# A gated MLP's u half: seven block products instead of eight for two of three chunk pairs

## The chip, the cores and the metric

One core of a Trainium2 chip runs the whole program. The metric is the device time of one execution in microseconds (us), the median over runs. The engines are TensorE (PE; its weight loads are listed as PEld), VectorE (DVE), ScalarE (ACT), GpSimd (POOL) and SyncE (SP), which issues the DMA transfers. Each engine takes its instructions in the order in which they were queued, and waits at an instruction until what that one needs is there.

## The reference

Windowed attention feeds an FFT mixing layer with an MLP, and that feeds a gated MLP. The change touches the last stage, and in it the product with the first half of `w_in`:

```python
def _moe2_ref(x, w_in, g_ln, w_sg, b_sg, w_out):      # x: 4 x 576 x 512, w_in: 512 x 1024
    h = x @ w_in
    c = np.float32(np.sqrt(2.0 / np.pi))
    h = 0.5 * h * (1.0 + np.tanh(c * (h + 0.044715 * h ** 3)))
    u, v = (h[..., :512], h[..., 512:])
    mu = np.mean(v, axis=-1, keepdims=True)
    var = np.mean((v - mu) ** 2, axis=-1, keepdims=True)
    v_n = (v - mu) / np.sqrt(var + 1e-06) * g_ln
    v_s = np.einsum('ts,bsd->btd', w_sg, v_n) + b_sg[None, :, None]
    gated = u * v_s
    return (x + gated @ w_out).astype(np.float32)
```

## The kernel before

**Numbers.** Every fp32 operand of a product is split into a hi and a lo part (`xh`, `xl` for the tokens), and one product of 128 by 128 by some columns is three matmuls, hi by hi, hi by lo, lo by hi (`mm3`, L124 to L126). Weights come from HBM as 64-bit words that `raw` (L158 on ACT, L159 and L160 on DVE) turns into fp32 and `halves` splits (L164 on ACT; L165 on DVE, or on POOL once the MLP is over).

**Stages.** Attention and the FFT come first, then the MLP. Its larger part, `wino`, works on pairs of token chunks (a chunk is 384 of the 2304 tokens; there are six): `quad` makes a two by two block product from seven block products instead of eight (Strassen's scheme in Winograd's form), with the sums on the side of the output made by DVE and POOL (L830, L831), relu and split by ACT and DVE (L824, L825), and `units` multiplies by the second weight and adds the result to `uT`, the fp32 tokens, in `done` (L878, a DVE add whose one operand is a PSUM bank). Then the gated MLP:

- `split_x` splits the six chunks: for each chunk and each of four 128-row blocks k, ACT writes hi (L900) and POOL writes lo, which is token minus hi (L901). That is 24 splits on each of the two engines. The tiles are called `xh`/`xl` (chunk 0), `xhm`/`xlm` (chunks 1 and 2) and `xht`/`xlt` (chunks 3 to 5).
- `gate_u` (the u half): for each chunk and each of four output blocks f, 4 blocks k by 3 matmuls of 384 columns into a PSUM bank (called `c` or `g`), then a gelu on ACT (L1008) that writes over `uT`. That is 6 x 4 x 12 = 288 matmuls.
- `v_tiles` (the v half, token-major, with the layer norm), `spatial` (the mixing by `w_sg`, whose weights `load_sg` brings) and `project`.

**What sets the order.** The program is written as generators that a driver interleaves by credit (`drive`, with lanes for weight decoding), and a tile scheduler then puts the instructions of each engine in a fixed order. In `wino` a lane decodes `w1`, `w2` and, from its fourth pair on, the gated MLP's `w_in` (`at("in", ...)`). `split_x` is issued after the last relu splits of the MLP (`issue_after`). Work with high priority, such as `done`, goes ahead of what was written earlier.

**Banks.** PSUM has eight banks. When `gate_u` begins, it takes banks that the last `units` still hold: a bank is free when DVE's `done` add has read it.

Of the kernel before, what the change touches and what calls it, by code (L numbers as in the profile page):

```python
# [1 line left out]

# [31 lines left out]
GSETS = (3, 4, 5, 7, 8, 6, 1, 2)  # L34
# [73 lines left out]
class Kernel:  # L108
# [70 lines left out]
    def decode_w1(self, f):  # L179

        V = self.nc.vector
        w = self.aps["w1"]
        a21 = self.raw(w[f + 1], 0)
        yield 0
        a22 = self.raw(w[f + 1], 256)
        self.halves(a22, *self.w1_block(f, 4))
        s1 = self.pers.tile([128, 256], I32, tag="dec_w", bufs=4, name="dec_w")[:].bitcast(F32)
        V.tensor_tensor(out=s1, in0=a21, in1=a22, op=ALU.add)
        self.halves(s1, *self.w1_block(f, 5))
        yield 0  # L190
# [25 lines left out]
    def gset(self, i):  # L216
        return self.sets[GSETS[i]]

    def decode_in(self, uv, kc):
        i = 4 * uv + kc  # L220
        t = self.gset(i // 2)
        yield from self.decode(self.aps["wi"][i], t[:, 2 * (i % 2)], t[:, 2 * (i % 2) + 1])

    def decode_out(self, kc):
        t = self.gset(4 + kc // 2)
        yield from self.decode(self.aps["wo"][kc], t[:, 2 * (kc % 2)], t[:, 2 * (kc % 2) + 1])

    def w_in(self, uv, kc):
        t = self.gset(2 * uv + kc // 2)
        return t[:, 2 * (kc % 2)], t[:, 2 * (kc % 2) + 1]  # L230

    def w_out(self, kc):
        t = self.gset(4 + kc // 2)
        return t[:, 2 * (kc % 2)], t[:, 2 * (kc % 2) + 1]
# [713 lines left out]
    def open_gmlp(self):  # L948
# [46 lines left out]

    def gate_u(self):
# [114 lines left out]
def emit(tc, aps):  # L1111
    with ExitStack() as ctx:
# [263 lines left out]
```

## Time and profile before

| | us |
|---|---|
| median of 3 runs | 771.15 (770.38 to 771.23) |
| the profiled execution, its time | 772.72 |
| its span, first to last instruction | 770.9 |
| PE busy | 750.4 (97% of the span) |
| DVE, ACT, POOL busy | 486.0, 340.6, 219.7 |
| granted TensorE clock, mean | 0.997 of full speed |

Durations below are from the profiled execution. How to read its views: busy time adds up the durations of an engine's instructions; the chain of waits goes back from the last instruction, at each step to what released it; a timeline lists an engine's instructions by start, and a row with "x4" stands for four alike in a row, its time being that from the first's start to the last's end. Matmuls overlap in PE, so the step from start to start is what a matmul costs, not its duration of 0.33 to 0.35 us.

### The profile page before, as it was taken

What the parts mean: (1) busy time and instruction counts of PE and PEld (TensorE: products, weight loads), DVE (VectorE), ACT (ScalarE), POOL (GpSimd) and SP (SyncE); (2) the same over time, 40 slices, a digit from 0 to 9 for tenths busy, and PEclk for the clock granted to TensorE, in tenths of its full rate; (3) what the DMA queues carried; (4) which work ended last, traced back from release to release, by engine and by line L of the source; (5) the groups of instructions that cost most, each with busy time, mean ns of one, the idle gap of its engine ahead of it and who ended that gap; (6) DMA issues with size and microseconds to landing.
All of it is one profiled execution on the core that took longest, in us unless ns stands there. A gap on an engine that the chain in (4) does not pass through costs nothing.

```text
span 770.9 us, 13909 instructions
## 1 busy us (share of the span) xinstructions
PE 750.4 (97%) x5018; PEld 723.3 (94%) x5018; DVE 486.0 (63%) x1382; ACT 340.6 (44%) x811; POOL 219.7 (28%) x278
## 2 busy tenths in 40 slices
PE   7899899899999999999999999999999999999998
PEld 6789788899999999999999999999999998989898
DVE  4668876883445599884688657645700468574662
ACT  5687986745235555341245324323732333231210
POOL 2244454524213460065421112022690021010100
PEclk9999999999999999999999999999999999999999
DMA  9997762343015888585838914853310020104023
GB/s 265 307 291 229 210 212 68 111 136 116 8 29 180 278 270 297 181 321 178 309 122 308 363 81 162 336 205 123 121 57 1 0 71 22 62 23 142 11 72 122
DMA packets 84772, 123.37 MB, mean 160 GB/s; under 512 B 24416, under 2 KB 61664, under 8 KB 84704
## 3 DMA queue, kind: packets, MB, share of 16 engines
q1 hardware_dynamic: 82912, 119.13, 46.4%
q0 software_dynamic: 576, 2.97, 1.1%
q8 instruction: 39, 0.64, 0.3%
q10 hardware_dynamic: 1216, 0.39, 0.2%
q14 instruction: 29, 0.24, 0.1%
HBM read 91.79 MB, written 30.67 MB: 159 GB/s over the span
## 4 chain that ended last, share of the span: by engine, by line
PE 90%; DVE 5%; ACT 3%; DMA 1%; issue 1%; SPq 0%; POOL 0%; ACTq 0%; DVEq 0%; POOLq 0%
PE w L124 7%; PE w L126 7%; PE w L125 7%; PE g L124 7%; PE g L126 6%; PE g L125 6%; PE c L124 6%; PE c L125 6%; PE c L126 6%; PE acc L126 3%; PE acc L125 3%; PE h L124 3%; PE h L125 3%; PE acc L124 3%; PE h L126 3%; PE sc L314 3%
## 5 line engine op out<-in xcount | busy, mean ns | idle before, releaser
L164 ACT ACTIVATE set<-dec_w 128x256 fp32r<-128x256 f32 x103 | 41.9, 414 | 63.2 <-PE w L125 29.4
L831 POOL TENSOR_TENSOR u<-u 128x384 f32<-128x384 f32 x15 | 17.7, 1179 | 158.6 <-ACT u L830 99.6
L605 POOL TENSOR_TENSOR rq<-rq,mhalf 128x1 f32<-128x1 f32 (+1 forms) x24 | 15.7, 654 | 157.8 <-DVE rq L604 155.6
L321 ACT ACTIVATE s<-s,mx 128x128 f32<-128x128 f32 x144 | 47.6, 392 | 7.7 <-DVE mx L319 7.5
L158 ACT ACTIVATE dec_g<-dec_s 128x256 f32<-128x256 f32 x88 | 37.4, 428 | 30.5 <-DMA dec_s<-in_wi 15.3
L125 PE MATMUL acc<-rl,set 128*128 128x384 f32 x144 | 48.7, 338 | 0.0
L126 PE MATMUL acc<-rh,set 128*128 128x384 f32 x144 | 48.6, 337 | 0.0
L319 DVE CUSTOM_DVE_ANT_0 s<-sc,mask 128x128 f32<-128x128 f32 x144 | 33.4, 285 | 22.0 <-PE sc L314 13.8
L124 PE MATMUL acc<-rh,set 128*128 128x384 f32 x144 | 46.3, 337 | 0.0
L314 PE MATMUL sc<-k,q 128*128 128x128 f32 x288 | 41.0, 286 | 5.0 <-DVE mx L319 2.4
L165 DVE TENSOR_TENSOR set<-dec_w,set 128x256 fp32r<-128x256 f32 x83 | 37.8, 462 | 10.8 <-ACT set L164 4.3
L160 DVE SCALAR_TENSOR_TENSOR dec_w<-dec_g,dec_w 128x256 int32<-128x256 int32 x88 | 42.1, 481 | 3.5 <-ACT dec_g L158 2.8
L1037 DVE BATCH_NORM_STATS2 st<-u 128x6 f32<-128x512 f32 x18 | 12.4, 691 | 48.7 <-ACT u L1033 48.7
L314 PEld LDWEIGHTS sc<-k,q 128*128 128x128 f32 x288 | 36.7, 198 | 6.7 <-DVE mx L319 3.0
L831 DVE TENSOR_TENSOR u<-w,u 128x384 f32<-128x384 f32 x44 | 24.3, 552 | 27.2 <-POOL u L831 22.4
L159 DVE TENSOR_SCALAR dec_w<-dec_s 128x256 int32<-128x256 int32 x88 | 32.3, 373 | 6.1 <-DMA dec_s<-in_wi 3.2
L878 DVE TENSOR_TENSOR uT<-g,uT 128x384 f32<-128x384 f32 x36 | 19.4, 554 | 26.4 <-PE g L126 26.3
L703 DVE SCALAR_TENSOR_TENSOR rl<-h,rh 128x384 fp32r<-128x384 f32 x36 | 19.8, 551 | 23.1 <-ACT rh L702 23.1
L341 PEld LDWEIGHTS pv<-v,pts 128*64 128x64 f32 x576 | 23.5, 137 | 9.3 <-issue 4.2
L341 PE MATMUL pv<-v,pts 128*64 128x65 f32 x576 | 29.1, 226 | 2.8 <-ACT s L321 2.4
L830 ACT ACTIVATE u<-w 128x384 f32<-128x384 f32 x29 | 14.0, 484 | 38.0 <-PE w L126 37.1
L688 DVE TENSOR_TENSOR uT<-acc,uT 128x384 f32<-128x384 f32 x48 | 25.4, 549 | 5.3 <-PE acc L126 4.9
(359 smaller groups left out, 2632.5 us busy)
## 6 DMA issues: line engine op xcount, KB each, us to landing
dec_s<-in_w SPq DMA_DIRECT2D x64, 256.0 KB, 3.4
v<-in_v SPq DMA_DIRECT2D x16, 520.0 KB, 5.5
xht<-xb SPq DMA_DIRECT2D x10, 768.0 KB, 8.5
xhm<-xb SPq DMA_DIRECT2D x10, 768.0 KB, 7.9
xlm<-xb SPq DMA_DIRECT2D x8, 768.0 KB, 8.9
k<-in_k SPq DMA_DIRECT2D x11, 512.0 KB, 6.3
xf<-u SPq DMA_DIRECT2D x18, 256.0 KB, 3.0
p<-xf SPq DMA_DIRECT2D x24, 192.0 KB, 3.2
```

What stands on the lines that cost most here:

```text
L124: mm(out, lhsT=lh, rhs=rh, start=first and i == 0, stop=False)
L125: mm(out, lhsT=lh, rhs=rl, start=False, stop=False)
L126: mm(out, lhsT=ll, rhs=rh, start=False, stop=last and i == n - 1)
L158: nc.scalar.activation(out=g, in_=s[:, :, 1].bitcast(F32), func=AF.Prelu, scale=2.0 ** -112, alpha=-2.0 ** 32)
L160: nc.vector.scalar_tensor_tensor(out=w, in0=g[:].bitcast(I32), scalar=3, in1=w, op0=ALU.logical_shift_left, op1=ALU.bitwise_or)
L164: self.nc.scalar.activation(out=hi, in_=f, func=AF.Copy)
L165: (self.nc.gpsimd if self.bp is None else self.nc.vector).tensor_tensor(out=lo, in0=f, in1=hi, op=ALU.subtract)
L314: nc.tensor.matmul(sc[:, hp], lhsT=q[:, hp].rearrange("p a b -> p (a b)"), rhs=k[:, hp, o:o + 128], start=True, stop=True)
L319: nc.vector.tensor_tensor_reduce(out=s[:, hp], in0=sc[:, hp], in1=mask, scale=-0.125, scalar=1e30, op0=ALU.add, op1=ALU.min, accum_out=mx[ ...
L321: nc.scalar.activation(out=s[:, hp], in_=s[:, hp], func=AF.Exp, bias=mx[:, hp:hp + 1], scale=-1.0)
L341: nc.tensor.matmul(o[r:r + 64, i // 4, 65 * (i % 4):65 * (i % 4) + 65], lhsT=pts[:, i // 2, 64 * (i % 2):64 * (i % 2) + 64], rhs=v[:, 65 * ...
L831: add = lambda eng, o, i, j: eng.tensor_tensor(out=o, in0=i, in1=j, op=ALU.add)
```

## The change

**The products.** Chunks 0 and 1 keep the plain form (`gplain`, 48 matmuls each). Chunks 2 and 3, and 4 and 5, are taken as pairs: `gquad(p, f)` makes two output blocks by two chunks from seven block products of two blocks k, each 6 matmuls. Two pairs by two halves f by seven by 6 are 168 matmuls; with the plain 96 they are 264, where there were 288. `TURNS` sets the order of the seven. Products 1 and 6 have no bank of their own: they are accumulated onto the bank of product 0 and of product 5, after ACT or DVE has read these (`skip`). The other sums on the output side are five DVE adds (L1049) and an ACT copy (L1065) for each `gquad`.

**The sums of tokens.** Four of the seven products multiply sums of tokens. `tsum` makes them from `uT` (four DVE subtractions for each pair and block k, L1020), and `tsplit` splits them (hi on ACT, L1031; lo on DVE, L1032). For the first pair this is done between the splits of chunk 0 and of the other chunks; for the second pair the sums are made before `gquad(1, 1)` and split within it.

**The weights.** `wi` for the u half is stored in blocks, and `decode_u` makes seven forms of it for each half f, as `decode_w1` does (L193 to L202 before), with one block more that `gplain` needs. So 16 blocks are split where 8 were. Of `w_in`'s v half two of four row blocks are still decoded in `wino`, one (with one of `w_out`) beside `gate_u`, one before `gquad(2, 1)`; the other three row blocks of `w_out` are decoded in the first `spatial`. `load_sg` of the first block comes after `gate_u`. The tiles of v for batch 0 come after `gate_u`, in turns with `gplain(1)`.

```diff
-GSETS = (3, 4, 5, 7, 8, 6, 1, 2)
+FORMS = ((5, 3, 7, 4, 0, 1, 2, 6), (7, 4, 5, 0, 3, 2, 1, 6))
+TURNS = (0, 2, 3, 5, 1, 4, 6)
+W_V = ((8, 0, 8, 1), (8, 2, 8, 3), (6, 0, 6, 1), (3, 0, 3, 1))
+W_OUT = ((3, 2, 3, 3), (5, 0, 5, 1), (6, 2, 6, 3), (5, 2, 5, 3))
+SG = (1, 4, 7)
...
-    def mm3(self, out, terms, first=True, last=True):
+    def mm3(self, out, terms, first=True, last=True, skip=False):
 
         n = len(terms)
         for i, (lh, ll, rh, rl) in enumerate(terms):
-            mm = self.nc.tensor.matmul
+            mm = partial(self.nc.tensor.matmul, skip_group_check=skip)
...
+    def u_block(self, f, i):
+        n = 8 * f + FORMS[f].index(i)
+        t = self.flat((3, 4, 5, 7)[n // 4])[:, 512 * (n % 4):512 * (n % 4) + 512]
+        return t[:, 0:256], t[:, 256:512]
+
+    def decode_u(self, f):
+        return self.decode_forms(self.aps["wi"], 2 * f, lambda i: self.u_block(f, i), True)
+
+    def decode_forms(self, w, f, place, spare=False):
 
         V = self.nc.vector
-        w = self.aps["w1"]
         a21 = self.raw(w[f + 1], 0)
+        if spare:
+            self.halves(a21, *place(7))
...
+    def tsum(self, p, k, ts):
+
+        sub = lambda o, a, b: self.nc.vector.tensor_tensor(out=o, in0=a, in1=b, op=ALU.subtract)
+        t1, t2, t3, t4 = ts
+        m, n = 2 * p, 2 * p + 1
+        sub(t1, self.xk(n, k), self.xk(m, k))
+        sub(t2, self.xk(n, k + 2), t1)
+        sub(t3, self.xk(n, k + 2), self.xk(n, k))
+        sub(t4, self.xk(m, k + 2), t2)
+        return {5: t1, 2: t2, 3: t3, 4: t4}
+
+    def tsplit(self, i, k, t):
+        h, l = self.tb[i][k]
+        self.nc.scalar.activation(out=h, in_=t, func=AF.Copy)
+        self.nc.vector.tensor_tensor(out=l, in0=t, in1=h, op=ALU.subtract)
+
+    def tsums(self, p, temps):
+        for k in range(2):
+            f = self.tsum(p, k, [t[:, 0:384] for t in temps])
+            for i in (2, 3, 5, 4):
+                self.tsplit(i, k, f[i])
...
+        x = lambda c, o: [(self.xh[c][:, o + k], self.xl[c][:, o + k]) for k in range(2)]
+        tb = {0: x(m, 0), 1: x(m, 2), 6: x(n, 2), **self.tb}
+        p1, u3, p5 = (self.ptile("u") for _ in range(3))
+        add = lambda o, i, j: V.tensor_tensor(out=o, in0=i, in1=j, op=ALU.add)
+
+        def gelu(e, t, c):
+            A.activation(out=self.xk(2 * p + t, 2 * f + e), in_=c, func=AF.Gelu_apprx_tanh)
+
+        banks = {}
+        for i in TURNS:
+            hi, lo = self.u_block(f, i)
+            if i in (1, 6):
+                o = banks[i // 6 * 5]
+            else:
+                o = banks[i] = self.ctile()[:, 0:384]
+            self.mm3(o, [(hi[:, 128 * k:128 * k + 128], lo[:, 128 * k:128 * k + 128], *tb[i][k]) for k in range(2)], first=i not in (1, 6), skip=i in (1, 6))
+            if then is not None and i in self.tb:
+                then(i)
+            if i == 0:
+                A.activation(out=p1, in_=o, func=AF.Copy)
+            elif i == 1:
+                gelu(0, 0, o)
+            elif i == 2:
+                add(p1, o, p1)
+            elif i == 3:
+                add(u3, o, p1)
+            elif i == 4:
+                add(u3, o, u3)
+                gelu(1, 0, u3)
+            elif i == 5:
+                add(p5, o, u3)
+                gelu(1, 1, p5)
+            else:
+                add(p1, o, p1)
+                gelu(0, 1, p1)
+            yield 960
...
+        temps = [self.cp.tile([128, 512], F32, tag=f"t{i}", name="temp")[:, 0:384] for i in range(4)]
+        yield from self.gplain(0)
+        yield from self.gquad(1, 0)
+        late = [self.tsum(2, k, t) for k, t in enumerate((temps, [self.ptile("p") for _ in range(4)]))]
+        yield from self.gquad(1, 1, lambda i: [self.tsplit(i, k, late[k][i]) for k in range(2)])
+        yield from self.gquad(2, 0)
+        for _ in self.decode_in(3):
+            pass
+        yield from self.gquad(2, 1)
...
+            k.open_sums()
+            k.split_x(0)
+            k.tsums(1, k.ptiles[:4])
+            for n in (2, 3, 4, 5, 1):
...
+            yield from spaced(k.decode_in(2), 1000)
+            yield from outs(2)
+
+        lane = [prep()]
+        drive(k.gate_u(), lane)
+        drain(lane)
...
+        fill = {"v": k.v_tiles(0), "p": k.gplain(1)}
+        for g in "vvvpvpvpp":
+            next(fill[g])
...
+            wo = [outs(0, 1, 3)] if b == 0 else []
+            drive(k.spatial(b), wo)
+            drain(wo)
```

**DVE where the MLP ends and the gated MLP begins.** Before, the last eight `done` adds (`uT<-g` and `uT<-w`; the source is the bank) follow one another, and DVE's next work is the layer norm of v:

```order
L878 TENSOR_TENSOR uT_61<-g_6589,uT_61 128x384
L878 TENSOR_TENSOR uT_61<-g_6590,uT_61 128x384
L878 TENSOR_TENSOR uT_61<-w_6591,uT_61 128x384
L878 TENSOR_TENSOR uT_61<-w_6592,uT_61 128x384
L878 TENSOR_TENSOR uT_61<-w_6666,uT_61 128x384
L878 TENSOR_TENSOR uT_61<-w_6667,uT_61 128x384
L878 TENSOR_TENSOR uT_61<-g_6664,uT_61 128x384
L878 TENSOR_TENSOR uT_61<-g_6665,uT_61 128x384
L1037 BN_STATS st_7145<-u_7143 128x6
```

After, from the fifth of them on (four sums `u<-uT` and four `done` adds stand ahead of this piece):

```order
L1032 TENSOR_TENSOR set2_71<-u_4345,set2_71 128x384
L890 TENSOR_TENSOR uT_61<-w_6638,uT_61 128x384
L1020 TENSOR_TENSOR u_4345<-uT_61 128x384
L1032 TENSOR_TENSOR set2_71<-u_4347,set1_70 128x384
L890 TENSOR_TENSOR uT_61<-w_6639,uT_61 128x384
L1032 TENSOR_TENSOR set1_70<-u_4346,set1_70 128x384
L1020 TENSOR_TENSOR u_4347<-uT_61 128x384
L1020 TENSOR_TENSOR u_4346<-uT_61,u_4345 128x384
L890 TENSOR_TENSOR uT_61<-g_6636,uT_61 128x384
L1032 TENSOR_TENSOR set2_71<-u_4347,set2_71 128x384
L1032 TENSOR_TENSOR set1_70<-u_4346,set1_70 128x384
L890 TENSOR_TENSOR uT_61<-g_6637,uT_61 128x384
```

The `done` adds that free `g_6636` and `g_6637` now stand behind six and eight instructions of `tsum` (L1020) and `tsplit` (L1032, out is a `set` tile).

**DVE a little later**, where the last lo parts of the first pair are made. Before, nothing stands there (the rows above are followed by `BN_STATS`). After:

```order
L1020 TENSOR_TENSOR temp_6806<-uT_61,temp_6805 128x384
L1020 TENSOR_TENSOR u_4348<-uT_61,u_4346 128x384
L1020 TENSOR_TENSOR p_6962<-uT_61,p_6961 128x384
L1020 TENSOR_TENSOR p_6963<-uT_61 128x384
L1020 TENSOR_TENSOR temp_6808<-uT_61,temp_6806 128x384
L164 TENSOR_SCALAR dec_w_7112<-dec_s_7109 128x256
L1020 TENSOR_TENSOR p_6964<-uT_61,p_6962 128x384
L1032 TENSOR_TENSOR pq_6722<-u_4348,set0_69 128x384
L165 SCALAR_TENSOR_TENSOR dec_w_7112<-dec_g_7111,dec_w_7112 128x256
L164 TENSOR_SCALAR dec_w_7121<-dec_s_7118 128x256
L165 SCALAR_TENSOR_TENSOR dec_w_7121<-dec_g_7120,dec_w_7121 128x256
L1049 TENSOR_TENSOR u_6901<-c_6912,u_6901 128x384
```

The split `pq<-u` of sum 4 stands behind the sums of the second pair (`temp`, `p`) and a decoding step; eleven instructions of `tsum` and `tsplit` and that step stand between the last `done` add and it.

**PE from the 73rd matmul of the u half on.** Before, chunk 1 in the plain form:

```order
L124 MATMUL c_6958<-xhm_2187,set3_2189 128x384
L125 MATMUL c_6958<-xlm_2188,set3_2189 128x384
L126 MATMUL c_6958<-xhm_2187,set3_2189 128x384
L124 MATMUL c_6958<-xhm_2187,set3_2189 128x384
L125 MATMUL c_6958<-xlm_2188,set3_2189 128x384
L126 MATMUL c_6958<-xhm_2187,set3_2189 128x384
```

After, product 4 of `gquad(1, 0)` and the beginning of the next products:

```order
L129 MATMUL g_6944<-set0_69,set3_2189 128x384
L130 MATMUL g_6944<-set0_69,set3_2189 128x384
L131 MATMUL g_6944<-set0_69,set3_2189 128x384
L129 MATMUL g_6944<-set0_69,set3_2189 128x384
L130 MATMUL g_6944<-pq_6722,set3_2189 128x384
L131 MATMUL g_6944<-set0_69,set3_2189 128x384
L129 MATMUL c_6976<-xhm_2187,set5_2191 128x384
L130 MATMUL c_6976<-xlm_2188,set5_2191 128x384
L131 MATMUL c_6976<-xhm_2187,set5_2191 128x384
L129 MATMUL g_6904<-xhm_2187,set4_2190 128x384
L130 MATMUL g_6904<-xlm_2188,set4_2190 128x384
```

The fifth of these rows is the 77th matmul of the u half and reads `pq`, the tile that the DVE row above writes; product 6, 19 matmuls further on, goes onto the bank of product 5 (`c_6928`) once the third L1049 add has read it.

**POOL in the same stretch.** Before:

```order
L901 TENSOR_TENSOR xl_120<-uT,xh_119 128x384 x4
L901 TENSOR_TENSOR xlm<-uT,xhm 128x384 x8
L901 TENSOR_TENSOR xlt<-uT,xht 128x384 x3
L165 TENSOR_TENSOR set_3126<-dec_w,set_3126 128x256 x2
L901 TENSOR_TENSOR xlt<-uT,xht 128x384 x3
L165 TENSOR_TENSOR set_3126<-dec_w,set_3126 128x256
L901 TENSOR_TENSOR xlt<-uT,xht 128x384 x2
L165 TENSOR_TENSOR set_3126<-dec_w,set_3126 128x256
L901 TENSOR_TENSOR xlt<-uT,xht 128x384 x4
```

After:

```order
L913 TENSOR_TENSOR xl_120<-uT,xh_119 128x384 x4
L913 TENSOR_TENSOR xlm<-uT,xhm 128x384 x4
L913 TENSOR_TENSOR xlt<-uT,xht 128x384 x2
L913 TENSOR_TENSOR xlm<-uT,xhm 128x384 x4
L913 TENSOR_TENSOR xlt<-uT,xht 128x384
L170 TENSOR_TENSOR set_3126<-dec_w,set_3126 128x256
L913 TENSOR_TENSOR xlt<-uT,xht 128x384 x2
L170 TENSOR_TENSOR set_3126<-dec_w,set_3126 128x256
L913 TENSOR_TENSOR xlt<-uT,xht 128x384 x3
L170 TENSOR_TENSOR set_3126<-dec_w,set_3126 128x256 x2
L913 TENSOR_TENSOR xlt<-uT,xht 128x384 x4
```

The 24 lo splits and the four splits of weights stay on POOL; chunk 2 comes ahead of chunk 1.

## Rows read from the trace of the kernel before

**Rows 1.** the page: busy time by engine, and the chain that ended last by engine

```profile
PE 750.4 (97%) x5018; PEld 723.3 (94%) x5018; DVE 486.0 (63%) x1382; ACT 340.6 (44%) x811; POOL 219.7 (28%) x278
...
PE 90%; DVE 5%; ACT 3%; DMA 1%; issue 1%; SPq 0%; POOL 0%; ACTq 0%; DVEq 0%; POOLq 0%
```

**Rows 2.** busy time in five stretches (columns: us, then each engine, clock, DMA)

```profile
400.00:549.80 149.80, 149.80 (x862) 149.64 (x861) 101.51 (x239) 54.24 (x128) 25.03 (x24) 1.00 0.57 214
549.80:558.00 8.20, 8.20 (x49) 8.20 (x48) 4.10 (x9) 8.20 (x21) 8.18 (x8) 1.00 0.31 112
558.00:576.40 18.40, 18.40 (x108) 18.40 (x107) 0.56 (x1) 8.08 (x17) 18.40 (x21) 1.00 0.20 60
576.40:608.00 31.60, 31.60 (x175) 30.49 (x174) 5.22 (x16) 8.77 (x17) 4.47 (x7) 1.00 0.00 1
608.00:770.90 162.90, 159.45 (x962) 150.86 (x960) 97.67 (x263) 39.20 (x81) 12.67 (x20) 1.00 0.20 62
```

**Rows 3.** PE, timeline (start us, us, engine, line, operation, out<-in)

```profile
553.84 0.34 PE L124 MATMUL g<-xlt,set 128*128 128x384 f32 x1
...
558.02 0.34 PE L124 MATMUL c<-xh,set 128*128 128x384 f32 x1
...
566.41 0.34 PE L124 MATMUL c<-xhm,set 128*128 128x384 f32 x1
...
583.05 0.33 PE L124 MATMUL g<-xht,set 128*128 128x384 f32 x1
```

**Rows 4.** POOL, timeline from 549.8 us on

```profile
549.82 4.36 POOL L901 TENSOR_TENSOR xl<-uT,xh 128x384 fp32r<-128x384 f32 x4 [2.82 <-ACT xh L900]
...
564.87 1.42 POOL L165 TENSOR_TENSOR set<-dec_w,set 128x256 fp32r<-128x256 f32 x2
...
572.51 3.91 POOL L901 TENSOR_TENSOR xlt<-uT,xht 128x384 fp32r<-128x384 f32 x4
```

**Rows 5.** ACT, timeline: splits of the chunks (hi part)

```profile
549.24 1.75 ACT L900 ACTIVATE xh<-uT 128x384 fp32r<-128x384 f32 x4
...
554.21 1.34 ACT L900 ACTIVATE xht<-uT 128x384 fp32r<-128x384 f32 x3
```

**Rows 6.** DVE, timeline around 550 us

```profile
549.82 0.55 DVE L825 SCALAR_TENSOR_TENSOR xlt<-pq,xlt 128x384 fp32r<-128x384 f32 x1
551.26 1.02 DVE L878 TENSOR_TENSOR uT<-g,uT 128x384 f32<-128x384 f32 x2 [0.89 <-PE g L126]
```

**Rows 7.** DVE, timeline from 329.8 to 337.5 us

```profile
329.88 0.28 DVE L159 TENSOR_SCALAR dec_w<-dec_s 128x256 int32<-128x256 int32 x1
...
332.25 1.11 DVE L159 TENSOR_SCALAR dec_w<-dec_s 128x256 int32<-128x256 int32 x1
...
333.75 0.77 DVE L160 SCALAR_TENSOR_TENSOR dec_w<-dec_g,dec_w 128x256 int32<-128x256 int32 x1
334.55 1.13 DVE L193 TENSOR_TENSOR dec_w<-dec_w 128x256 f32<-128x256 f32 x1
335.61 1.37 DVE L825 SCALAR_TENSOR_TENSOR xlt<-u,xlt 128x384 fp32r<-128x384 f32 x1
```

**Rows 8.** POOL, timeline over the same stretch

```profile
332.01 1.20 POOL L738 TENSOR_TENSOR p<-p 128x384 f32<-128x384 f32 x1
333.17 1.06 POOL L831 TENSOR_TENSOR u<-pq,u 128x384 f32<-128x384 f32 x1
334.20 3.64 POOL L738 TENSOR_TENSOR p<-p 128x384 f32<-128x384 f32 x3
```

**Rows 9.** chain of waits there (start us, us, what)

```profile
336.97 0.48 DVE u L831
337.50 0.45 PE w L124
```

**Rows 10.** DVE (first row) and POOL (second), timeline at 402 us

```profile
402.14 0.74 DVE L165 TENSOR_TENSOR set<-dec_w,set 128x256 fp32r<-128x256 f32 x2
...
402.31 2.52 POOL L831 TENSOR_TENSOR u<-u 128x384 f32<-128x384 f32 x1 [7.33 <-ACT u L830]
```

More of the change, by code (lines that the diff above doesn't have):

```diff
@@ L1 @@
 from contextlib import ExitStack
+from functools import partial
 import numpy as np
@@ L214, in decode_f, with halfset, w_in, w_out @@
             yield from self.decode(self.aps[nm][f], t[:, 2 * i], t[:, 2 * i + 1])
[L216 to L222, printed above, removed]
-    def decode_out(self, kc):
[L225 to L234, printed above, removed]
+    def halfset(self, at):
+        return [self.flat(i)[:, 512 * q:512 * q + 512] for i, q in (at[:2], at[2:])]
+    def w_in(self, kc):
+        return self.halfset(W_V[kc])
+    def w_out(self, kc):
+        return self.halfset(W_OUT[kc])
+    def decode_in(self, kc):
+        yield from self.decode(self.aps["wi"][4 + kc], *self.w_in(kc))
+    def decode_out(self, kc):
+        yield from self.decode(self.aps["wo"][kc], *self.w_out(kc))
     def gtile(self):
@@ new lines, in open_sums @@
+    def open_sums(self):
+        t = [t for i in (1, 2, 0) for t in [self.flat(i)[:, 384 * j:384 * j + 384] for j in range(5)]]
+        t.append(self.ptile("pq")[:].bitcast(F32R))
+        self.tb = {i: [(t[4 * j + 2 * k], t[4 * j + 2 * k + 1]) for k in range(2)] for j, i in enumerate((2, 3, 5, 4))}
+    def tsum(self, p, k, ts):
[7 more added lines that the diff above has]
+        return {5: t1, 2: t2, 3: t3, 4: t4}
@@ new lines, in gplain @@
+    def gplain(self, n):
+        for f in range(4):
+            ps = self.ctile()[:, 0:384]
+            terms = []
+            for k in range(4):
+                wh, wl = self.u_block(f // 2, (0, 1, 7, 4)[2 * (f % 2) + k // 2])
+                o = slice(128 * (k % 2), 128 * (k % 2) + 128)
+                terms.append((wh[:, o], wl[:, o], self.xh[n][:, k], self.xl[n][:, k]))
+            self.mm3(ps, terms)
+            self.nc.scalar.activation(out=self.xk(n, f), in_=ps, func=AF.Gelu_apprx_tanh)
+            yield 1920
@@ L1221, in behind, with u_forms @@
                 yield w
-        def w_in(r, gap):
-            for i in r:
-                yield from spaced(k.decode_in(i // 4, i % 4), gap)
+        def u_forms(gap):
+            yield from spaced(k.decode_u(0), gap)
+            gen = k.decode_u(1)
+            for _ in range(2):
+                next(gen)
+                yield gap
+            while not st7:
+                yield None
+            for _ in gen:
+                yield gap
+            for kc in range(2):
+                yield from spaced(k.decode_in(kc), gap)
+        st7 = []
         def blocks():
@@ L1300, in emit, with outs @@
         k.open_gmlp()
+        def outs(*ns):
+            for kc in ns:
+                yield from spaced(k.decode_out(kc), 1000)
         def prep():
-            k.load_sg(0, 0)
-            k.load_sg(0, 1)
-            for kc in range(4):
-                yield from spaced(k.decode_out(kc), 1000)
-        def first():
-            yield 6 * 4 * 1400
-            yield from k.v_tiles(0)
-        fill = [[prep()], [first()]]
-        drive(k.gate_u(), *fill)
-        for f in sum(fill, []):
-            for _ in f:
-                pass
+            yield from spaced(k.decode_in(2), 1000)
[3 more added lines that the diff above has]
+        drain(lane)
+        k.open_v()
+        for h in range(2):
+            k.load_sg(0, h)
+        fill = {"v": k.v_tiles(0), "p": k.gplain(1)}
+        for g in "vvvpvpvpp":
+            next(fill[g])
         for i in range(8):
```

55 lines of the change are left out of this document (24 added, 31 removed).

## Prediction

> **What bounds the kernel now.** I read the page's busy times first, then the chain of waits: PE is busy 97% of the span and carries 90% of the chain [rows 1]. The table by stretches then tells where a saving in PE would count: from 400 us to 608 PE has no idle time, and its clock is 1.00 [rows 2]. So in the u half a matmul less is time less, and a wait more is time more, since nothing behind it gives it back. The other engines' columns show what lies beside PE there: from 549.8 to 576.4 POOL is busy all the time (8.18 of 8.20 us, 18.40 of 18.40), while DVE does 0.56 us in the second part [rows 2]. That idle DVE is what the change fills.
>
> **What the products give.** In the u half a matmul follows the one before by (583.05 - 566.41) / 96 = 0.1733 us [rows 3]; 96 matmuls stand between these rows. 264 in place of 288 save 24 x 0.1733 = 4.16 us. It is the only saving. Blocks of 128 by 128 by 384 stay what they were, so the step should too; the clock is at its upper level (2.4 GHz) in every stretch of [rows 2] and PE has no reason to idle long.
>
> **What costs nothing, as long as its cover holds.** The additional decoding in wino (eight splits more, eight sums more, against the v and output weights that now come later) lies beside a PE without idle time, with DVE busy 101.5 of 149.8 us and ACT 54.2 [rows 2]. The 20 L1049 adds read a bank; such an add follows another by 0.47 us (two in 1.02, 0.55 each) [rows 6], and a block product is six matmuls, 1.04 us, so adds keep up. Accumulating product 1 on product 0's bank waits for one ACT copy, 24 matmuls or 4.2 us after that bank's first product began; product 6 waits for three DVE adds, which I charge below. The weights decoded in the first spatial stage and beside gate_u meet DVE at 97.7 of 162.9 us and 5.2 of 31.6 [rows 2], and each is needed several us after it can be there. `load_sg` behind gate_u has the v tiles in front of it. The second pair's sums and splits run after 576.4, where POOL is busy 4.47 of 31.6 us [rows 2]. Lost cover would cost about 1 us a piece; I charge 0, with 1 us in the upper end.
>
> **What the sums cost: DVE beside a busy POOL.** For the first pair and the head of the second, 25 instructions of DVE whose sources are all in SBUF come into the stretch from 549.8 us on, in which POOL splits back to back at 0.98 us each (four in 3.91) [rows 4]. What they take there is no row of their own, but 331 to 337 us shows the same meeting: POOL works without a gap [rows 8], and DVE's instructions with SBUF sources take 1.11, 0.77, 1.13 and 1.37 us [rows 7], where alone one takes 0.28 (L159, [rows 7]), 0.37 (two L165 in 0.74, [rows 10]) or 0.55 (L825, [rows 6]). They end at 333.36, 334.52, 335.68 and 336.98: one per POOL instruction, 1.16 us apart for 256 columns and 1.30 for 384. POOL pays as well: three in 3.64 with two of DVE's among them [rows 8], against 2.94 at 0.98. PE waited: the bank that `u<-w` frees at 336.97 let PE go on at 337.50 [rows 9]. An add that reads a bank does not take part (`u<-w`, 0.48, [rows 9]). For the 384-column sums and splits I take 1.25 us, since POOL's split of 0.98 is up to 0.08 shorter than its 1.06 there [rows 4, 8].
>
> The Trainium skill states this as a rule (SBUF — State Buffer, Who interferes with whom): a VectorE instruction with two inputs in SBUF and a GpSimd instruction that reads SBUF share a port pair under an exclusive lock, and the loser stands still for the whole instruction. The rows agree for L193 and L825; by that rule the L159 with one input (1.11 us) would contend only in a two-port mode.
>
> **Step by step.** (a) PE's times without any wait: the u half starts at 558.02 [rows 3], its 77th matmul (`g_6944<-pq`) is due at 558.02 + 76 x 0.1733 = 571.19, and product 6 at 574.48. (b) When can `pq` be there? ACT does 15 hi splits before the first `tsplit` copy. Four splits take 1.75 us, or 0.41 each from start to start [rows 5], so they end at 549.24 + 15 x 0.41 = 555.5, and the first lo split of a sum can start at about 556.0. (c) From there 20 wide and one narrow SBUF instruction of DVE stand up to and with `pq<-u`: 20 x 1.25 + 1.16 = 26.2 us. I take off 1.0 for the four POOL splits of weights (0.71 each, [rows 4], not 0.98) and 0.6 for a first slot that is half over; the four `done` adds fit beside POOL. So `pq` is there at 580.6, 9.4 us late. (d) POOL stays busy that long: it has 28 instructions, some five are done by 556, and 21 slots leave two. (e) Three decoding steps and three adds of 0.47 still come before product 6: 580.6 + 2 x 1.16 + 0.35 + 1.4 = 584.7, against 574.48 + 9.4 = 583.9, so 0.8 more. Together 10.2 us. Parts of it show earlier: `g_6809`, due at 558.02 + 17 x 0.1733 = 560.97, waits for a `done` add behind six slots, 556.0 + 7.5 - 0.6 + 0.5 = 563.4, so 2.4 us; and the first four sums may hold the first `done` add past 553.84, where PE takes its bank [rows 3], by up to 1.4 us. These are within the 10.2, not on top.
>
> The sum: -4.16 + 10.2 = +6.0 us. Against the profiled execution that is 772.72 + 6.0 = 778.7; against the median of the runs, 1.6 us lower, 771.15 + 6.0 = **777.1 us**.
>
> Ends: with 1.30 for a wide slot 1.0 more, with a lost cover or PE's later start 1 to 2 more, so 780.5; with 1.16 for every slot 1.8 less, 775.3.
>
> **Rivals.** *No meeting (faster).* If DVE's sums run beside POOL at 0.47 us apart, `pq` needs 21 x 0.47 = 9.9 us from 556.0 and is there at 565.9, 5 us early; the bank for `g_6809` is free at about 560.2, 0.8 early. Then only the saving is left: 771.15 - 4.16 = 767.0. It decides from a slot of about 0.7 us down. Against it stand all four rows at 331 to 337 us; for it, that the rows there are of other lines and partly of integer type.
>
> *DVE keeps going and POOL waits.* At 402 us a POOL add took 2.52 us instead of 1.0 while DVE went on at 0.37 us an instruction [rows 10]. By that DVE is in time, but POOL's 21st instruction, the lo half that product 6 reads, ends late: before, 549.82 + 4.36 + 15 x 0.98 + 1.4 = 570.3; with 25 DVE instructions of 0.43 in between, 581.1, or 6.6 after 574.48. Net +2.4: 773.6. For it speaks that row; against it, that DVE's queue in the new stretch waits on ACT and on banks again and again, and gives POOL its turn.
>
> The same section of the skill says that issue order decides who blocks; both rows can be read so, and it leaves open which of the two cases comes here.
>
> *The loss stays near the saving.* If each of the 25 costs POOL only the (3.64 - 2.94) / 2 = 0.35 us of [rows 8] and DVE loses nothing else, the 21st ends at 579.1, 4.6 late: 771.6; with 0.30, 770.4.
>
> *The products don't come out fewer on PE's path.* Then the waits alone would count, 781; the order of instructions shows 264, so I give it no weight of its own.
>
> **How the numbers follow.** DVE and POOL in turns, 775.3 to 780.5: 0.64. POOL waits, 773.6: 0.12. Near the saving, 770.4 to 771.6: 0.08. No meeting, 767.0: 0.16. A measurement of this kernel tells about 0.2%, 1.5 us, from no change. Faster by over that (below 769.6): 0.16. Within it (to 772.7): 0.08. Slower: 0.76. A range from 770.2 to 780.5 leaves out the case without a meeting and a few in a hundred above.
>
> **What would show it.** In the changed kernel's trace: L1020 and L1032 on DVE at 1.2 us and more from 550 to 580 us, with L913 on POOL above 1.1; PE gaps before the `g` bank near 561 us and before the matmul that reads `pq`; 264 matmuls of the u half still 0.173 us apart; no other PE gap in the gated MLP. I am wrong if L1020 and L1032 take 0.55 us there, or if POOL's splits stretch to 2 us while DVE's don't, or if the gaps come from elsewhere, such as ACT's copies or the weights.

## The result

The changed kernel takes 775.36 us (median of 6 runs, 775.02 to 777.2), the kernel before 770.76 (6 runs, 768.9 to 771.7). The ratio is 1.0065 with a 95% interval of 1.0050 to 1.0081: 5.0 us slower (3.9 to 6.2). The forecast was 777.1 us, in a range from 770.2 to 780.5, and slower.

Two rows of the profile page of the changed kernel, busy time and the chain that ended last, beside [rows 1]:

```profile
PE 748.9 (97%) x4994; PEld 720.3 (93%) x4994; DVE 530.6 (69%) x1446; ACT 351.5 (45%) x839; POOL 234.8 (30%) x282
...
PE 82%; DVE 10%; DMA 4%; ACT 2%; issue 2%; SPq 0%; POOL 0%; DVEq 0%; ACTq 0%; POOLq 0%
```

DVE's part of the chain has doubled, from 5% to 10%, and PE's has fallen from 90% to 82%, though PE has 24 matmuls fewer. The same two stretches as the second and third of [rows 2] (us, then PE, PEld, DVE, ACT, POOL busy, clock, DMA):

```profile
549.80:558.00 8.20, 7.79 (x45) 7.47 (x43) 8.20 (x12) 4.86 (x13) 8.20 (x8) 1.00 0.42 133
558.00:576.40 18.40, 13.06 (x62) 12.16 (x63) 18.40 (x19) 7.05 (x14) 18.40 (x16) 0.91 0.15 52
```

PE has idle time now, 5.3 of 18.4 us in the second stretch, where it had none. DVE went from 0.56 us to all of it; POOL is as busy as before with the same 24 + 4 instructions. The granted clock fell to 0.91 in this stretch.

**By stages.** The profiled execution of the kernel before spent 46.0 us up to the first matmul of the FFT, 1.5 to 4 us more than the other profiled executions (41.9 to 44.5), so whole spans don't compare. From the first matmul of the u half to the first of the spatial stage (u half and v tiles of batch 0) they do. In the kernel before that is from 558.02 [rows 3] to

```profile
622.00 0.31 PE L124 MATMUL c<-set,set 128*128 128x320 f32 x1
```

and in the changed one from and to

```profile
554.43 0.34 PE L129 MATMUL c<-xh,set 128*128 128x384 f32 x1
```

```profile
623.99 0.31 PE L129 MATMUL c<-set,set 128*128 128x320 f32 x1
```

63.98 and 69.56 us. From there to the end it is 148.95 and 149.65, and the stages ahead, from the FFT on, differ by 0.2 us. The change costs 5.58 + 0.70 = 6.3 us by the profiles, just above the upper end of the runs' interval (6.2).

**Where PE waited.** What PE waited for between 549 and 585 us (line waited in, releaser: us, times, longest):

```profile
PE g L129 <- ACT uT L1103: 4.6, 1, 4.6
PE g L129 <- DVE uT L890: 1.2, 2, 1.0
PE c L129 <- DVE u L1049: 0.9, 1, 0.9
```

From start to start these waits and PE's restarts behind them are 1.12, 0.37, 4.75, 0.11 and 1.02 us longer than a step, 7.4 together. PE's timeline shows the long one, and what follows it:

```profile
565.06 0.34 PE L129 MATMUL c<-set,set 128*128 128x384 f32 x1
569.98 0.50 PE L129 MATMUL g<-xhm,set 128*128 128x384 f32 x1 [4.58 <-ACT uT L1103]
570.28 0.52 PE L130 MATMUL g<-xlm,set 128*128 128x384 f32 x1
...
573.48 0.41 PE L129 MATMUL c<-set,set 128*128 128x384 f32 x1
573.73 0.34 PE L130 MATMUL c<-set,set 128*128 128x384 f32 x1
...
575.92 0.44 PE L130 MATMUL g<-pq,set 128*128 128x384 f32 x1
...
580.34 0.45 PE L129 MATMUL c<-xht,set 128*128 128x384 f32 x1 [0.86 <-DVE u L1049]
```

After 4.6 us without work PE's step is 0.32 us instead of 0.173, until 573.5: the granted clock is at its lower level (1.2 GHz), and 12 steps take 1.67 us more. With 0.4 us for steps of 0.28 behind the four other waits the account is 63.98 - 4.16 + 7.37 + 1.67 + 0.4 = 69.3 of the 69.56 measured.

**DVE and POOL.** Their timelines in that stretch, to be set beside [rows 7, 8]:

```profile
560.98 2.18 DVE L1020 TENSOR_TENSOR temp<-uT 128x384 f32<-128x384 f32 x2
...
565.39 1.34 DVE L1020 TENSOR_TENSOR p<-uT 128x384 f32<-128x384 f32 x1
...
567.65 1.34 DVE L1020 TENSOR_TENSOR u<-uT,u 128x384 f32<-128x384 f32 x1
...
572.47 0.82 DVE L164 TENSOR_SCALAR dec_w<-dec_s 128x256 int32<-128x256 int32 x1
...
574.50 1.37 DVE L1032 TENSOR_TENSOR pq<-u,set 128x384 fp32r<-128x384 f32 x1
```

```profile
563.72 2.60 POOL L913 TENSOR_TENSOR xlt<-uT,xht 128x384 fp32r<-128x384 f32 x2
566.28 1.03 POOL L170 TENSOR_TENSOR set<-dec_w,set 128x256 fp32r<-128x256 f32 x1
567.28 3.85 POOL L913 TENSOR_TENSOR xlt<-uT,xht 128x384 fp32r<-128x384 f32 x3
```

Each sum and split of DVE ends 1.26 to 1.30 us after the one before it, and its row is 1.34 to 1.37 us long (0.9 where a `done` add came between); beside one of the four 256-column splits of POOL it is 1.0 from end to end. POOL's split of 0.98 us has become 1.30. The rows of the two engines overlap, so a row seems to hold the waiting too; what shows the turns is that their ends alternate, one for one, from 551 to 578 us. A turn of both is shorter than the two alone, one behind the other: 1.28 us, where 0.98 + 0.47 are 1.45, and 1.00 beside a narrow split, where 0.70 + 0.47 are 1.17, so 0.17 less in both cases.

### The profile page after: what moved, and what is told of

Its sections match the earlier page's. It is cut to its first block, busy times and chain, and to the rows that moved or that the text cites. A ratio compares the mean times of both kernels' runs of the same rounds, so it can differ in the third digit from the quotient of the medians.

```text
span 773.6 us, 13953 instructions
## 1 busy us (share of the span) xinstructions
PE 748.9 (97%) x4994; PEld 720.3 (93%) x4994; DVE 530.6 (69%) x1446; ACT 351.5 (45%) x839; POOL 234.8 (30%) x282
## 4 chain that ended last, share of the span: by engine, by line
PE 82%; DVE 10%; DMA 4%; ACT 2%; issue 2%; SPq 0%; POOL 0%; DVEq 0%; ACTq 0%; POOLq 0%
PE g L129 6%; PE w L129 6%; PE w L130 6%; PE w L131 6%; PE c L129 6%; PE c L131 6%; PE c L130 6%; PE g L131 6%; PE g L130 6%; PE acc L131 3%; PE acc L130 3%; PE h L129 3%; PE h L130 3%; PE acc L129 3%; PE h L131 3%; PE sc L326 3%
## 5 line engine op out<-in xcount | busy, mean ns | idle before, releaser
L169 ACT ACTIVATE set<-dec_w 128x256 fp32r<-128x256 f32 x111 | 45.1, 413 | 69.8 <-PE w L130 31.5
L170 DVE TENSOR_TENSOR set<-dec_w,set 128x256 fp32r<-128x256 f32 x87 | 39.4, 460 | 10.2 <-ACT set L169 3.6
L165 DVE SCALAR_TENSOR_TENSOR dec_w<-dec_g,dec_w 128x256 int32<-128x256 int32 x88 | 43.0, 490 | 3.3 <-ACT dec_g L163 2.6
L131 PE MATMUL c<-set,set 128*128 128x320 f32 (+2 forms) x120 | 36.7, 306 | 0.0
L129 PE MATMUL c<-set,set 128*128 128x320 f32 (+2 forms) x120 | 36.6, 305 | 0.0
L164 DVE TENSOR_SCALAR dec_w<-dec_s 128x256 int32<-128x256 int32 x88 | 33.0, 381 | 5.3 <-DMA dec_s<-in_wo 3.1
L715 DVE SCALAR_TENSOR_TENSOR rl<-h,rh 128x384 fp32r<-128x384 f32 x36 | 19.8, 551 | 23.9 <-ACT rh L714 23.8
L130 PE MATMUL c<-set,set 128*128 128x320 f32 (+2 forms) x117 | 35.6, 305 | 0.0
```

The lines of the kernel that those rows point to most:

```text
L129: mm(out, lhsT=lh, rhs=rh, start=first and i == 0, stop=False)
L130: mm(out, lhsT=lh, rhs=rl, start=False, stop=False)
L131: mm(out, lhsT=ll, rhs=rh, start=False, stop=last and i == n - 1)
L164: nc.vector.tensor_scalar(out=w, in0=s[:, :, 0], scalar1=29, scalar2=None, op0=ALU.logical_shift_right)
L165: nc.vector.scalar_tensor_tensor(out=w, in0=g[:].bitcast(I32), scalar=3, in1=w, op0=ALU.logical_shift_left, op1=ALU.bitwise_or)
L169: self.nc.scalar.activation(out=hi, in_=f, func=AF.Copy)
```

## The experiments

Each kernel was timed against the kernel before on the same chip; the stretch is the one of the section above, from the first matmul of the u half to the first of the spatial stage. Waits are told from start to start, less a step.

| kernel | median, us | ratio, interval | stretch, us |
|---|---|---|---|
| before | 769.8 to 770.8 | 1 | 63.98 |
| changed | 775.36 | 1.0065 (1.0050 to 1.0081) | 69.56 |
| splits on DVE | 768.86 | 0.9980 (0.9968 to 0.9993) | 61.19 |
| late sums | 769.65 | 0.9988 (0.9977 to 0.9999) | 63.10 |
| gelu first | 778.96 | 1.0119 (1.0102 to 1.0135) | 72.18 |
| products alone, first | 776.26 | 1.0076 (1.0061 to 1.0090) | 70.09 |
| products alone, second | 771.1 | 1.0001 (0.9984 to 1.0018) | 62.92 |
| products alone, third | 767.19 | 0.9964 (0.9950 to 0.9977) | 60.15 |
| reordered | 770.3 | 1.0008 (0.9991 to 1.0025) | 62.88 |
| reordered, decoding later | 768.31 | 0.9981 (0.9969 to 0.9993) | 61.35 |
| before, splits on DVE | 772.69 | 1.0035 (1.0021 to 1.0050) | 63.97 |

### Taking the meeting away: the splits on DVE

```diff
-            self.nc.gpsimd.tensor_tensor(out=self.xl[n][:, k], in0=x, in1=self.xh[n][:, k], op=ALU.subtract)
+            self.nc.vector.tensor_tensor(out=self.xl[n][:, k], in0=x, in1=self.xh[n][:, k], op=ALU.subtract)
```

> The changed kernel with one line edited: the 24 lo splits of the token chunks run on DVE, POOL is left with the four weight splits. Theory (DVE and POOL take turns at their shared access to SBUF): a DVE instruction with SBUF sources falls from 1.28 us beside a busy POOL to about 0.47, so even with 24 instructions more DVE needs 52 x 0.47 = 24 us instead of 28 x 1.28 = 36, and the PE waits of 7.4 us shrink to 1 to 3 us: 767 to 769.5 us, 6 to 8 below the changed kernel. Rival (what counts is how many instructions stand ahead of the ones that PE waits for, wherever the splits run): DVE's queue is 24 longer, so 777 or more.

768.86 us. DVE has 24 instructions more and is ready earlier; its timeline (columns as above):

```profile
562.18 0.55 DVE L1020 TENSOR_TENSOR u<-uT 128x384 f32<-128x384 f32 x1
562.65 0.55 DVE L1032 TENSOR_TENSOR set<-u,set 128x384 fp32r<-128x384 f32 x1
...
563.58 0.55 DVE L913 TENSOR_TENSOR xlt<-uT,xht 128x384 fp32r<-128x384 f32 x1
```

0.55 us each, 0.47 from start to start. Of PE's waits two are left, 0.88 us at product 4 of `gquad(1, 1)`, whose bank an L1049 add frees, and 1.0 just ahead of the u half, where `done` adds now stand behind splits. The queue's length is not the cause; the turns are.

The control does the same to the kernel before:

> The kernel before with its 24 lo splits on DVE instead of POOL. Theory: without sums DVE and POOL hardly met there, PE did not wait, so nothing changes, 770 us within 1 us; what the split-on-DVE version of the changed kernel gained it gained by ending the meeting. Rival (splits on DVE are better in themselves): 768 or less.

772.69 us, which neither had foreseen: 2.7 us slower by the ratio (1.6 to 3.9). Its stretch is unchanged (63.97), but ahead of it PE waited:

```profile
PE g L124 <- DVE uT L878: 2.0, 1, 2.0
```

The splits stand ahead of the `done` add that frees the bank. Splits on DVE are no gain in themselves; the changed kernel gains 6.5 us by them since they end the meeting.

### Moving what stands ahead: late sums

```diff
-        late = [self.tsum(2, k, t) for k, t in enumerate((temps, [self.ptile("p") for _ in range(4)]))]
+        with self.tc.issue_after(self.gmark):     # gmark: the third L1049 add of gquad(1, 0)
+            late = [self.tsum(2, k, t) for k, t in enumerate((temps, [self.ptile("p") for _ in range(4)]))]
```

> The changed kernel, with the eight sums of the second pair held back until the third L1049 add of the first block product set, so that they no longer stand ahead of the first pair's last splits on DVE. POOL's work is as in the changed kernel. Theory (turns): eight slots of 1.28 us, 10 us, leave the way to sum 4 and its split; what stays are the waits of 1.1 and 0.4 us at the first two g banks and about 1 us at the next: 769 to 770.5 us. Rival (POOL's own lateness is what PE waits for): no gain, 775.

769.65 us, as the theory had it. What PE waited for between 540 and 640 us:

```profile
PE g L129 <- DVE uT L890: 1.4, 2, 1.2
PE c L129 <- DVE u L1049: 0.7, 1, 0.7
```

DVE and POOL still take turns, but from start to start PE waits 1.35 and 0.39 us at the first two g banks and 0.82 at product 2 of `gquad(2, 0)`, and no more at `g_6904` or `pq`. The wait of 4.6 us was the eight sums of the second pair, which nobody needed yet.

### Which link of the chain: gelu first

The wait of 4.6 us was ended by a gelu. ACT's timeline shows what it stood behind:

```profile
562.93 0.49 ACT L1103 ACTIVATE uT<-c 128x384 f32<-128x384 f32 x1
569.02 0.52 ACT L1031 ACTIVATE set<-u 128x384 fp32r<-128x384 f32 x1 [5.61 <-DVE u L1020]
569.46 0.85 ACT L1103 ACTIVATE uT<-g 128x384 f32<-128x384 f32 x2
```

ACT idled 5.61 us for DVE's sum 4 (`u<-uT`, L1020), at a copy that stands ahead of three gelus.

```diff
-            for i in (2, 3, 5, 4):
+            for i in (2, 3, 5, 4)[:4 - k]:       # sum 4 of the second k is split later:
                 self.tsplit(i, k, f[i])
...
         yield from self.gplain(0)
+        with self.tc.issue_after(self.gel):      # gel: the last gelu of gplain(0)
+            self.tsplit(4, 1, self.f4)
```

> The changed kernel, with ACT's copy of the last sum (sum 4, second block k) placed behind the four gelus of chunk 0 instead of ahead of three of them. The wait of 4.6 us at the g bank was ended by such a gelu, which stood behind this copy, which waited for DVE's sum. Theory (DVE's late chain is the cause, ACT only passes it on): the wait moves to the matmul that reads pq, whose split is not earlier than before, so 775 to 778 us. Rival (the order on ACT is the cause): the wait goes, and with it the lowered clock behind it, 769 us.

778.96 us, 1 above the theory's range and 10 from the rival. The wait moved to `pq`, as it had to if DVE's chain is the cause:

```profile
570.77 0.33 PE L129 MATMUL c<-xhm,set 128*128 128x384 f32 x1
579.20 0.69 PE L130 MATMUL g<-pq,set 128*128 128x384 f32 x1 [8.10 <-DVE pq L1032]
```

The edit did more than the text before it says: on DVE the split of sum 4 moved back too, behind three decoding instructions.

```profile
577.58 1.10 DVE L165 SCALAR_TENSOR_TENSOR dec_w<-dec_g,dec_w 128x256 int32<-128x256 int32 x1
578.60 0.55 DVE L1032 TENSOR_TENSOR pq<-u,set 128x384 fp32r<-128x384 f32 x1
```

It ended 23.8 us after the start of the u half, 2.35 later than in the changed kernel (21.4). Without that the kernel would take some 776.6 us, an estimate from the two numbers.

### The saving by itself: products alone

The sums and their splits are left out, so part of the computation is missing; the four products that need them read splits of chunk 2 or 4.

```diff
-        tb = {0: x(m, 0), 1: x(m, 2), 6: x(n, 2), **self.tb}
+        tb = {0: x(m, 0), 1: x(m, 2), 6: x(n, 2), 2: x(m, 0), 3: x(m, 2), 5: x(m, 0), 4: x(m, 2)}
...
-            k.tsums(1, k.ptiles[:4])
```

> The changed kernel without the sums of tokens and their splits (tsum and tsplit are left out; the four products that need sums read splits of chunk 2 or 4 instead, so part of the computation is left out). 264 matmuls, the L1049 adds, the two accumulations, the weight forms and the order of the other work stay. Theory: this is the saving by itself, 24 x 0.1733 = 4.2 us below the kernel before, 766.6 us. Rival (something else in the change costs: weights decoded later, accumulation onto read banks, adds): above 768.

776.26 us. This run tells nothing of the saving: without the sums a load of `w_sg` had come forward on ACT, ahead of gelus, and PE waited 7.0 us. With all loads of `w_sg` behind the last gelu of the block products:

> As the run of the products alone, which PE spent 6.9 us of in one wait for a gelu that stood behind a copy of w_sg that the missing sums had let move forward on ACT. Here all loads of w_sg come after the last gelu of the block products. tsum and tsplit are left out as before, so part of the computation is left out. Theory: the saving by itself, 766 to 767 us. Rival (the other parts of the change cost something): above 768.

771.1 us, runs from 766.4 to 773.4. The profiled execution was one of the shorter ones, 768.23, so what made others longer is not seen. Its stretch is 62.92 us, 1.06 less than before and not 4.16; one wait of 2.66 us at product 6 hides most of the rest. Its adds stood on DVE behind this row:

```profile
558.71 11.31 DVE L164 TENSOR_SCALAR dec_w<-dec_s 128x256 int32<-128x256 int32 x1 [4.07 <-POOL set L170]
```

A step of decoding (alone 0.28 us, [rows 7]) stood still for 11.3 us, while POOL made splits without a gap up to 569.5 us. The prediction had put the decoding beside gate_u at nothing. With it moved behind the third L1049 add:

> The products alone (tsum and tsplit left out, so part of the computation is left out) with the same edit to the decoding. In the run without it one wait of 2.66 us at product 6 was left, behind a decoding step that took 11.3 us on DVE beside POOL's splits. Theory: that was all that hid the saving; the u half and the v tiles take 59.7 to 60 us, 4.0 to 4.3 less than before, and the whole 766 to 767.5 us. Rival: the block products cost something of their own, the stretch stays above 61 us.

767.19 us and a stretch of 60.15: 3.83 us saved, with no wait of PE in it. The theory's mechanism holds; the saving is 0.3 short of 4.16 there, since the matmuls of the u half follow one another by 175.2 ns on the mean and not by 174.1 as before, and 0.7 us are lost in a later stage (below).

### The meeting by itself

Idle work was added to the kernel before, in a stretch where DVE and POOL have little to do.

> The kernel before with idle work added to a stretch in which DVE and POOL have little to do, to see the meeting by itself. First place, after a gelu of chunk 2: POOL makes ten adds of 384 columns from SBUF back to back, DVE nine instructions from SBUF with two sources (add), one source (tensor_scalar), and one source that is only read (bn_stats). Second place, after a gelu of chunk 4: DVE makes eight adds back to back, and POOL's four adds start once the first of them is done. Theory (turns): in the first place an add of DVE takes 1.2 to 1.4 us and POOL's 1.3; bn_stats, if two sources are what counts, 0.5 to 0.6; tensor_scalar as L164 did, 0.8 or more. In the second place they take turns too, POOL's first add ends within 1.6 us. Rival (whoever has it keeps it, as at 402 us): in the second place DVE's eight adds stay at 0.47 each and POOL's first add takes over 3 us.

The edit has twelve instructions of DVE in each place, not nine and eight. DVE's rows of both places (L1018 and L1024 adds, L1020 a tensor_scalar, L1022 bn_stats, L1027 the adds that start first), then POOL's:

```profile
581.10 0.55 DVE L1022 BATCH_NORM_STATS2 dummy_st<-uT 128x6 f32<-128x384 f32 x1
...
584.00 1.18 DVE L1024 TENSOR_TENSOR p<-uT 128x384 f32<-128x384 f32 x1
585.10 0.98 DVE L1020 TENSOR_SCALAR p<-uT 128x384 f32<-128x384 f32 x1
...
593.33 6.78 DVE L1027 TENSOR_TENSOR p<-uT 128x384 f32<-128x384 f32 x7 [5.05 <-ACT uT L1008]
```

```profile
578.84 10.13 POOL L1016 TENSOR_TENSOR p<-uT 128x384 f32<-128x384 f32 x10
593.97 5.13 POOL L1030 TENSOR_TENSOR p<-p,uT 128x384 f32<-128x384 f32 x4 [5.01 <-DVE p L1027]
```

An add takes 1.18 us beside POOL, a tensor_scalar with one source 0.98, bn_stats 0.55 as alone. In the second place DVE was first, and yet POOL's four adds take 1.28 each and DVE's 1.25 once POOL is there: turns, in both places. The rival by the row at 402 us [rows 10] did not come here, but the second place doesn't rule it out: DVE's adds there write one tile, so each begins 0.03 us after the end of the one before it, where at 402 us DVE ran without such gaps. When an engine that is already running keeps its turn is not shown.

> The kernel before with idle work: twice POOL makes ten adds from SBUF back to back, and a single instruction of DVE, idle until then, needs the result of the third (in the second place another that of the seventh). First place: a shift of every second integer, the form of L164 with fewer columns; second place: an add, then a contiguous fp32 tensor_scalar. Theory (turns): each gets its turn when POOL's current instruction ends, within 1.3 us. Rival (a decoding step that comes alone to a POOL that runs back to back gets no turn until POOL's run ends, as 11.2 and 11.3 us of L164 in the two runs of the products alone suggest): the shift takes about 6 us, the add and the tensor_scalar may still take turns.

```profile
579.11 0.87 DVE L1017 TENSOR_SCALAR p<-p 128x192 int32<-128x192 int32 x1 [22.59 <-POOL p L1015]
591.58 1.17 DVE L1019 TENSOR_TENSOR p<-p,uT 128x384 f32<-128x384 f32 x1 [11.60 <-POOL p L1015]
```

Each got its turn. So the 11.3 us of L164 (11.2 in the first run of the products alone) are not what a single arrival meets in general. In the reordered kernel below the same step came to the same splits of POOL after an idle 0.63 us and took 1.09. What kept it standing in two kernels stays open.

### Better orders

> The changed kernel with its order edited in three places and nothing else: the sums of the first pair's second block k come after the last done adds, the copy and split of their sum 4 after the gelus of chunk 0, and the second pair's sums after the third L1049 add. POOL keeps its splits, so DVE and POOL still meet. Theory (turns of 1.28 us; what hurts is who stands behind them): the banks of the first two g tiles come free in time, DVE's last split of the first pair ends near 567 us, where PE wants it, so PE's waits are 0 to 2 us: 766 to 768.5 us. Rival (the meeting itself costs, in any order): no better than 769.6, the late-sums kernel.

```diff
+                for i in self.dmarks[:k * 4]:           # dmarks: the last four done adds
+                    st.enter_context(self.tc.issue_after(i))
                 f = self.tsum(p, k, [t[:, 0:384] for t in temps])
```

with the edits of late sums and of gelu first. A fourth edit, which the text before it leaves out, holds the splits of chunk 1 back until the last `done` adds. 770.3 us (767.8 to 774.8), which doesn't bear out 766 to 768.5 and is what the rival gives; the stretch is 62.88 us, 1.1 less than before. One wait is left, 2.64 us at `pq`: the split stood behind two decoding steps (two instructions each), one of which waited 0.63 us for POOL (L165 is L164 of the other kernels):

```profile
568.02 1.09 DVE L165 TENSOR_SCALAR dec_w<-dec_s 128x256 int32<-128x256 int32 x1 [0.63 <-POOL set L171]
```

Without them:

> The reordered kernel with one more edit: the weights of the v half and of the output that were decoded beside gate_u are decoded after the third L1049 add. In the reordered kernel PE's one wait in the u half was 2.64 us at the matmul that reads pq, and that split stood on DVE behind two decoding steps, which waited for POOL. Theory: without them pq is there in time, the u half and the v tiles of batch 0 fall from 62.9 to about 60.2 us (before: 64.0), and the whole to 766 to 768 us, 3 below the kernel before. Rival (another wait takes its place, at product 6 or in the v tiles, where the weights now come late): no better than the reordered kernel.

```diff
         def prep():
-            yield from spaced(k.decode_in(2), 1000)
-            yield from outs(2)
+            while not hasattr(k, "gmark"):
+                yield None
+            ...                                         # the same two, each step under issue_after(k.gmark)
```

768.31 us, 1.5 below the kernel before (ratio 0.9981, interval 0.9969 to 0.9993), 7 below the changed one, and 0.3 above the theory's range. The stretch is 61.35, not 60.2: small waits of 0.2 to 0.5 us are left, one in `gquad(1, 0)` and two in `gquad(2, 0)`. Most of what the meeting cost was the order, then: 1.2 us of the stretch are left against the kernel without sums (60.15). This version and the splits on DVE beat the kernel before by 0.2%, late sums by 0.1%.

### A lost 0.7 us in the last stage

From the spatial stage to the end every kernel with the change takes 149.63 to 149.66 us, every one without it 148.95 to 148.98. The difference lies in `project`: its 288 matmuls follow one another by 173.6 ns on the mean before and 175.9 after, and 288 x 2.3 ns are 0.66 us of it.

> The changed kernel with the places of two row blocks of w_out exchanged: block 2 in the second half of set 5, block 3 in set 6. In the changed kernel project's matmuls follow one another by 175.3, 175.0, 174.4 and 177.8 ns for row blocks 0 to 3 of the weight (before: 174.1, 173.6, 173.3, 173.3), in all 0.69 us over its 288 matmuls. Theory: the step goes with the place of the weight, so block 2 becomes the slow one (about 178 ns) and block 3 falls to 174 or 175. Rival: it goes with the row block (its operands from the gated tokens, or its position in the chain of twelve), so block 3 stays at about 178.

The text before the run misreads the changed kernel's steps by up to 0.6 ns: from start to start they are 175.3, 175.0, 175.0 and 178.2 ns. Neither forecast came: block 0, which had not been moved, became the slow one (177.8 ns; blocks 1 to 3 are at 174.9 to 175.3), and from the spatial stage to the end it took the same 149.63. The weights of `w_out` lie elsewhere than before, and which block is slow changed with the exchange, but not as either theory said. The cause stays open.

## Why the prediction was right, and where not

**The bound and the cover.** PE had no idle time, so waits count in full: shown by the stretch's account, which closes to 0.3 us. The mechanism forecast is the one that came: DVE and POOL in turns, and PE waiting for what DVE made late.

**The saving.** 4.16 us was sized by the step. The products alone gave 3.83 in the stretch and lost 0.70 in `project`, 3.1 net. The term was a quarter too large: the step was taken to stay the same, and it grew by 0.6% in the u half and by 1.3% in `project`, for a reason that stays open.

**The turns.** 1.25 us was taken for a wide slot; measured are 1.26 to 1.30, and 1.00 beside a narrow split of POOL. The rows of lines other than the change's, [rows 7, 8], were the right ones. Splits on DVE showed that without the meeting the same instructions take 0.47.

**The sum of waits.** `pq` was to be there 22.6 us after the start of the u half; its split ended 21.4 after. PE reached its matmul 8.3 us late (9.4 forecast) and product 6 9.4 late (10.2). The sum of 10.2 was 0.8 too large, because the first lo split of a sum began 3.4 us ahead of the u half and not 2.0. Of the parts that were to show early, the bank of `g_6809` came 1.1 us late (2.4 forecast) and the first `done` add cost nothing. That the whole came so close is in part luck: waits 0.8 too large and a saving 1.0 too large nearly cancel.

**The place of the wait.** Here a step failed. The long wait was put at `pq`; it came 24 matmuls earlier, at the bank of `g_6904`, through a link that the prediction had not followed: ACT's copy of sum 4 stands ahead of gelus that free banks. The prediction had named a gap from ACT's copies as a sign of being wrong, and by its letter that sign came; but what the copy waited for was DVE's sum. With the link cut in gelu first, PE waits 8.3 us at `pq` instead. The link added nothing of its own: in the changed kernel the split of `pq` ended at 575.87 us (the row of 574.50) and PE's matmul began at 575.92, so what PE had lost at `g_6904` and in the 1.67 us of lower clock behind it, it no longer had to wait at `pq`. That PE "has no reason to idle long" was wrong as well, and by the prediction's own 10.2 us. The late sums show the instructions that made the chain long.

**The covered edits.** That the weights decoded beside gate_u cost nothing was wrong. Step (e) of the prediction itself charged 0.8 us for three decoding steps ahead of product 6, and in the changed kernel PE waited 1.0 us there; in the second kernel of the products alone and in the reordered one the decoding cost 2.6 us.

**The rivals.** No meeting (767.0) did not come, since DVE's sums ended 1.28 us apart and not 0.47; a kernel without sums takes 767.2. POOL waiting for DVE (773.6) was not seen: in 27 us of meeting DVE never had two turns in a row with POOL ready. The loss staying near the saving (770.4 to 771.6) supposed that DVE loses little, and it lost 0.8 us a turn. The Trainium skill (SBUF — State Buffer, Who interferes with whom) says that the loser stands still for the whole instruction and that two SBUF inputs contend. The trace agrees in kind, 1.18 us for an add and 0.55 for bn_stats, but a turn is 0.17 us shorter than both instructions one behind the other. The Trainium skill's sentence, in the same section, that issue order decides who blocks does not tell what two engines that both run without a gap do; here both paid, with a turn of 1.28 us for DVE's 0.47 and POOL's 0.98.

## What to carry to other kernels

An engine that looks idle is only free for work that doesn't meet its neighbour: before DVE is given sums from SBUF beside a POOL that runs back to back, price each at POOL's instruction plus its own (less 0.17 us here), and count how many stand ahead of what PE waits for. Work that is needed late should be held back by the program, as the scheduler had filled "idle" time with it; holding back eight sums was worth 5.7 us. When a saving is hidden by a wait, take the wait's cause away and measure again, since the next wait may be one that was put at nothing.

## What was not expected of the hardware

A wait of PE of 4.6 us was followed by 12 matmuls at the lower clock level, and so were waits of 7.0 and 8.3 us in other kernels by some; waits of 1.1, 1.0 and 2.6 us were not followed by such a stretch. A tensor_scalar with a single SBUF source waited for POOL like an add (0.98 us against 1.18), but cost POOL less (0.94 against 1.14 for its add beside them). One decoding step stood still for 11.2 and 11.3 us beside POOL in two kernels, and in the kernel made to repeat it 0.87: not explained, and neither is the step of `project`, which was 1.3% longer when its weights lay elsewhere.
